# Last stage of a spectral-layer backward pass: half-width inverse DFT sums, interleaved layer-norm rows, x reloaded elsewhere

## The chip, the cores and the metric

One core of one Trainium2 chip. The metric is the device time of one execution in microseconds (us); lower is better. The kernel was tuned already, so changes of one or two per cent count, and an execution's own spread (364.7 to 368.5 us over three batches of the kernel before) is of the size of the smaller effects. "PE" is TensorE, "PEld" its weight loads, "DVE" VectorE, "ACT" ScalarE, "POOL" GpSimd, "SP" SyncE, which issues the DMAs. A *cast* below is the copy of a PSUM result to SBUF in bf16.

## The reference

A residual block with two branches, and all of its gradients (shapes S = 2048 rows, D = 448 columns, F = 1792):

```python
h  = x + irfft2(rfft2(layernorm(x)) * (w_r + 1j * w_i))           # branch A, bf16
h2 = h + transpose(gelu(layernorm(layernorm(h)) @ w1 + b1) @ w2 + b2)   # branch B, mixes rows (cut: axes left out)
outputs = h2, and the gradients of x, w_r, w_i, w1, b1, w2, b2 for grad_out
```

What matters here is the end of the backward pass. The gradient of x needs an inverse DFT along the rows (sixteen tiles of 128 x 448), then the backward of the layer norm on each tile. Beside it the kernel does large matmuls for the gradients of w1 and w2 as *fill work*, handed to PE in small steps between the row work.

## The kernel before

Three pieces count. The row DFT gives four matmuls of 448 columns a tile, with `n_fill` steps of gradient work ahead of them:

```python
for s1 in range(NT):                       # NT = 16 row tiles
    if s1 + ahead_ < NT:
        q.append(first(s1 + ahead_))       # four 128-column matmuls and one cast prepare a later tile
    aT = q.pop(0)
    fill(n_fill)                           # n_fill = 8 gradient steps
    py = ps_ff()                           # a PSUM tile
    for i in range(4):                     # i // 2: cosine or sine part
        mm(py[:, 0:D], lhsT=aT[0:KC, i, :], rhs=csI[0:KC, i // 2, i % 2, :],
           start=(i == 0), stop=(i == 3))
    consumer(s1, py)
```

The consumer is the layer norm's backward, per tile one ACT operation, four DVE operations and small POOL operations on single columns:

```python
sc.activation(out=pb, in_=ps, func=ACT.Identity, scale=rstd, accum_out=ms)          # ACT, 448 columns
ve.tensor_tensor_reduce(out=tmp, in0=pb, in1=nrm, ..., accum_out=m2)                # DVE
...                                                                                 # cut: POOL works out s1, s2
ve.tensor_scalar(out=tmp, in0=nrm, scalar1=s2, scalar2=s1, op0=ALU.mult, op1=ALU.add)
ve.tensor_tensor(out=pb, in0=pb, in1=tmp, op=ALU.add)
ve.tensor_tensor(out=pb, in0=pb, in1=resid, op=ALU.add)                             # then stored, one tile a DMA
```

A cast goes to ACT or DVE, whichever has the lower load in a *cost model* that adds up an estimated duration for each operation as the program is built:

```python
def cost(self, name, n, bf16):
    if self.i == 0:                        # ACT
        return 0.17 + n / 1250.0
    if name in (..., "scalar_tensor_tensor", "tensor_tensor_reduce") or name == "tensor_copy" and not bf16:
        return 0.1 + n / 960.0             # DVE
    ...
    return 0.06 + n / (rate * (2.0 if bf16 else 1.0))
```

Of the kernel before, what the change touches and what calls it, by code (L numbers as in the profile page):

```python
# [13 lines left out]
ALU = mybir.AluOpType  # L14
# [3 lines left out]
P = 128  # L18
# [21 lines left out]
N_FILL_B = (16, 16, 40, 8, 24, 8)  # L40
# [10 lines left out]
class Meter:  # L51
# [10 lines left out]
    def cost(self, name, n, bf16):  # L62
        if self.i == 0:
            return 0.17 + n / 1250.0
        if name in ("bn_stats", "scalar_tensor_tensor", "tensor_tensor_reduce") or name == "tensor_copy" and not bf16:
            return 0.1 + n / 960.0
        rate = {"tensor_tensor": 960.0, "tensor_scalar": 1920.0, "tensor_copy": 1920.0}.get(name, 960.0)
        return 0.06 + n / (rate * (2.0 if bf16 else 1.0))

    def __getattr__(self, name):  # L70
        fn = getattr(self.eng, name)

        def run(**kw):
            ap = kw["in_"] if "in_" in kw else kw["in0"]
            n = int(np.prod(ap.shape[1:]))
            self.load[self.i] += self.cost(name, n, ap.dtype == BF16)
            low = max(self.load) - Meter.slack
            self.load[0], self.load[1] = max(low, self.load[0]), max(low, self.load[1])
            fn(**kw)  # L79
            side = Meter.side  # L80
            Meter.count += self.i
            if side and self.i == 1 and Meter.count % Meter.every == 0:
                Meter.side = ()
                side.pop(0)()
                Meter.side = side
        return run
# [33 lines left out]
def kernel(  # L120
# [634 lines left out]
    def inv_rows(consumer, n_fill, aTs, on_dve=()):  # L755
# [17 lines left out]
        for s1 in range(NT):  # L773
            if s1 + ahead_ < NT:
                q.append(first(s1 + ahead_))
            aT = q.pop(0)
            fill(n_fill)
            py = ps_ff()
            for i in range(4):
                mm(py[:, 0:D], lhsT=aT[0:KC, i, :], rhs=csI[0:KC, i // 2, i % 2, :],  # L780
                                 start=(i == 0), stop=(i == 3))
            consumer(s1, py)

    pending = []

    def fill(n):
        while n > 0 and pending:
            try:
                next(pending[0])
                n -= 1  # L790
            except StopIteration:
                pending.pop(0)

    def drain():
        while pending:
            fill(1)
# [367 lines left out]
    gp_.tensor_scalar(out=xcol[:, 2, :], in0=mvx[:, :, 0], scalar1=-1.0 / D, scalar2=None, op0=ALU.mult)  # L1164

    def ln_a(i, ps, rstd, nrm, m2scale):
# [3 lines left out]
        gp_.tensor_scalar(out=m1, in0=ms, scalar1=-1.0 / D, scalar2=None, op0=ALU.mult)  # L1170
        ve.tensor_tensor_reduce(out=tmp, in0=pb, in1=nrm, scale=-m2scale, scalar=0.0,
# [27 lines left out]
    ahead = []  # L1199

    def st_load():
        if order:
            reg, j = order.pop(0)
            st = st_ring.next()
            nc.sync.dma_start_transpose(out=st, in_=reg[:, j * 1024 + 64:j * 1024 + 960])
            ahead.append(st)


# [7 lines left out]
    for t in range(NT):  # L1216
# [10 lines left out]
        if t >= NT - 2:  # L1227
            st_load()
# [25 lines left out]
    def gw_gen(n, rhs, width, store, ost):  # L1254
        for u in range(n // 2):
            st = ahead.pop(0)
# [9 lines left out]
            def out(pw, w, c, i):  # L1266
# [3 lines left out]
                if x:  # L1270
                    if c == 3 and i:
                        st_load()
                    defer(1.5, lambda j=2 * u + i: store(j, 512 * (c - 1), x + w, o), o)

            for c in range(0, 4, 2):
# [14 lines left out]
                for i in range(2):  # L1290
                    for k in range(3):
                        whole(pv, w, c + 1, i, k, False, k == 2)
                        if k == 2:
# [7 lines left out]
                          Ring(ring(rG, 0, 8, S // 2).views + ost.views)))  # L1301
    load_W(3)
    for t in range(NT - LAG, NT + 2):
        if t == NT - 2:
            fill(8)
        rows(t)
# [7 lines left out]
    xall = cut(rX, 0, NT, D)  # L1314

    def load_xall(q):
        nc.sync.dma_start(out=xall[:, 4 * q:4 * q + 4, :], in_=x_pt[:, 4 * q:4 * q + 4, :])

    load_xall(0)
    load_xall(1)  # L1320

    X_AT = {3: 2, 7: 3}
    GW_AT = (4, 9, 11, 11, 12, 13, 14, 15)

    def gx_consumer(t, py):
# [4 lines left out]
        pb, tmp, m1, m2, ms = ln_a(NT + t, py[:, 0:D], rstd_x[:, t:t + 1], xall[:, t, :], 1.0 / D)  # L1330
        u, s2, s1 = (gcol[:, t, k:k + 1] for k in range(3))
        nmean, rstd2, md = (xcol[:, k, t:t + 1] for k in range(3))
        gp_.tensor_scalar(out=u, in0=ms, scalar1=md, scalar2=None, op0=ALU.mult)
        gp_.tensor_scalar(out=s2, in0=m2, scalar1=u, scalar2=rstd2, op0=ALU.subtract, op1=ALU.mult)
        gp_.tensor_scalar(out=s1, in0=s2, scalar1=nmean, scalar2=m1, op0=ALU.mult, op1=ALU.add)
        gx_todo.append((t, pb, tmp, s1, s2))
        if len(gx_todo) > 1:
            gx_finish()

    gx_todo = []  # L1340

    def gx_finish():
        t, pb, tmp, s1, s2 = gx_todo.pop(0)
        ln_b(pb, tmp, s1, s2, xall[:, t, :], dh[:, t, :], pb)
        defer(2.0, lambda: nc.sync.dma_start(out=out_1[0].rearrange("(p t) d -> p t d", t=NT)[:, t, :], in_=pb), pb)

    inv_rows(gx_consumer, N_FILL_B[5], aT_ring)
    while gx_todo:
        gx_finish()
    drain()  # L1350
    for _ in g_out:
        pass
# [30 lines left out]
```

## Time and profile before

366.0 us (median of three, 365.92 to 366.91). The span, first to last instruction, is 365.5.

| | before |
|---|---|
| PE busy, share of the span | 348.1 us, 95% |
| DVE busy | 262.2 us, 72% |
| ACT busy | 206.0 us, 56% |
| last stage starts, PE (first group of 128-column matmuls) | 309.89 us |
| last matmul group ends | 360.30 us |
| tail from there to the end of the span | 5.2 us |

The slices, stretches and chain are read in the prediction. One line of the page that it did not use matters afterwards. It is the clock that PE was granted, in tenths of full speed, one digit for each fortieth of the span:

```profile
PEclk9699998999999999999999999999999999999999
```

The 8 in the seventh slice (54.8 to 64.0 us, the eye takes it for noise) is a stretch of 3.41 us at half clock: in the clock record 1.00 is granted until 60.31, 0.50 until 63.73 and 1.00 after it.

### The profile page before, as it was taken

Reading aid. Unit: us, or ns where it says so; the run is one execution under the profiler, and the core shown is the slowest. Engines: PE = TensorE matmul, PEld = TensorE weight load, DVE = VectorE, ACT = ScalarE, POOL = GpSimd, SP = SyncE. Lnnn points to the kernel's source line nnn. Section 1 sums busy time; section 2 is a strip of 40 time slices with the busy share of each in tenths; the row PEclk is TensorE's granted clock in tenths of the full one; section 3 lists DMA queues with packets and bytes.
Section 4 is the critical chain, followed back from the end, with each engine's and each line's share of the span. In section 5 each row is a group of like instructions: output and inputs, shape, how many; then the busy total and the mean of one; then the engine's idle time right before and its main releaser. Section 6 shows DMA issues by size and latency. Waiting matters only on the chain.

```text
span 365.5 us, 6419 instructions
## 1 busy us (share of the span) xinstructions
PE 348.1 (95%) x2133; PEld 184.5 (50%) x2133; DVE 262.2 (72%) x677; ACT 206.0 (56%) x427; POOL 70.4 (19%) x226
## 2 busy tenths in 40 slices
PE   6798997899999999999999999999999999999994
PEld 2365764555645555555555555543444444455541
DVE  5898738882884888594237887874787884589882
ACT  4668834965986454512222455564577674676662
POOL 8676000000220000001001111100000000376760
PEclk9699998999999999999999999999999999999999
DMA  8999999647999999976868999969578899788897
GB/s 201 285 197 242 192 204 187 133 119 255 279 292 360 305 339 225 256 223 193 207 162 168 200 166 245 193 185 230 184 204 225 231 203 266 233 224 268 191 216 244
DMA packets 148825, 81.63 MB, mean 223 GB/s; under 512 B 95608, under 2 KB 140920, under 8 KB 148536
## 3 DMA queue, kind: packets, MB, share of 16 engines
q1 hardware_dynamic: 148792, 81.23, 91.7%
q8 instruction: 16, 0.26, 0.3%
q14 instruction: 17, 0.14, 0.1%
HBM read 27.56 MB, written 23.89 MB: 141 GB/s over the span
## 4 chain that ended last, share of the span: by engine, by line
PE 81%; ACT 5%; DVE 4%; DMA 3%; issue 2%; POOL 2%; SPq 1%; ACTq 0%; DVEq 0%
PE ps_mm L215 66%; PE ps_ff L215 15%; DMA rO<-in_B_w_dram 2%; ACT rO L79 2%; ACT rG L79 1%; DMA rA<-in_A_x_dram 1%; DVE stats L79 1%; DVE r L79 1%; SPq L294 1%; ACT Ut L79 1%; DVE rA L79 1%; ACT rX L79 0%; DVE rS L79 0%; POOL nt_f L383 0%; ACT rAT L79 0%
## 5 line engine op out<-in xcount | busy, mean ns | idle before, releaser
L215 PEld LDWEIGHTS <-r 128*128 128x128 bf16 (+1 forms) x628 | 59.9, 105 | 49.2 <-issue 2.0
L215 PEld LDWEIGHTS <-rS 128*128 128x128 bf16 (+2 forms) x528 | 42.9, 98 | 41.4 <-issue 9.2
L1170 POOL TENSOR_SCALAR lcol<-lcol 128x1 f32<-128x1 f32 x32 | 18.0, 562 | 148.4 <-ACT r L79 148.4
L215 PE MATMUL ps_mm<-rD,r 128*128 128x448 bf16 x224 | 44.5, 352 | 0.0
L215 PE MATMUL ps_mm<-rC,rE 128*128 128x448 bf16 x144 | 36.2, 369 | 3.7 <-DMA rC<-in_grad_out_dram 3.1
L215 PEld LDWEIGHTS <-rst 128*128 128x128 bf16 (+1 forms) x320 | 23.8, 97 | 29.0 <-issue 13.2
L79 ACT CAST rO<-ps_mm 128x512 bf16<-128x512 f32 (+1 forms) x52 | 28.5, 583 | 14.6 <-PE ps_mm L215 12.7
L79 ACT CAST r<-ps_ff 128x452 bf16<-128x452 f32 x53 | 30.5, 577 | 8.4 <-PE ps_ff L215 7.8
L215 PE MATMUL ps_mm<-rG,rst 128*128 128x512 bf16 (+1 forms) x160 | 35.0, 380 | 0.0
L215 PE MATMUL ps_mm<-rB,r 128*128 128x448 bf16 x160 | 31.2, 352 | 0.1
L215 PE MATMUL ps_mm<-r,rst 128*128 128x512 bf16 (+3 forms) x160 | 31.2, 353 | 0.0
L79 DVE CAST rO<-ps_mm 128x512 bf16<-128x512 f32 (+1 forms) x28 | 18.1, 658 | 10.4 <-PE ps_mm L215 10.3
L215 PE MATMUL ps_ff<-csI,rAT 113*128 113x448 bf16 x108 | 24.9, 353 | 0.4 <-ACT rAT L79 0.2
L79 DVE SCALAR_TENSOR_TENSOR r<-ps_mm,b2col,r 128x448 bf16<-128x448 f32 x16 | 10.9, 682 | 19.9 <-PE ps_mm L215 18.1
L79 ACT ACTIVATE r<-ps_mm,rstd_h 128x448 bf16<-128x448 f32 x16 | 10.1, 633 | 26.1 <-PE ps_mm L215 26.1
L79 ACT ACTIVATE r<-rC 128x448 bf16<-128x448 bf16 x16 | 9.1, 571 | 26.7 <-DMA out_dram<-r 19.3
L215 PEld LDWEIGHTS <-rO 128*128 128x128 bf16 (+1 forms) x165 | 15.8, 99 | 13.1 <-DMA rO<-in_B_w_dram 2.5
L215 PE MATMUL ps_mm<-rC,rO 128*128 128x448 bf16 x80 | 20.0, 366 | 2.2 <-DMA rO<-in_B_w_dram 2.2
L79 ACT ACTIVATE rG<-rG 128x896 bf16<-128x896 bf16 x14 | 13.3, 950 | 14.9 <-DVE rG L79 14.7
L215 PE MATMUL ps_mm<-rE,rS 128*128 128x448 bf16 x112 | 21.5, 352 | 0.0
L79 ACT CAST rS<-ps_ff 128x512 bf16<-128x512 f32 x31 | 18.3, 589 | 3.9 <-PE ps_ff L215 3.7
L215 PEld LDWEIGHTS <-rE 128*128 128x128 bf16 x148 | 14.2, 100 | 11.9 <-issue 4.8
(191 smaller groups left out, 634.4 us busy)
## 6 DMA issues: line engine op xcount, KB each, us to landing
out_dram<-rO SPq DMA_DIRECT2D x34, 256.0 KB
r<-in_B_w_dram SPq DMA_DIRECT2D x5, 1024.0 KB
r<-r SPq DMA_DIRECT2D x16, 226.0 KB
r<-r SPq DMA_DIRECT2D x32, 113.0 KB
rS<-in_B_w_dram SPq DMA_DIRECT2D x4, 896.0 KB
out_dram<-r SPq DMA_DIRECT2D x32, 112.0 KB
out_dram<-rG SPq DMA_DIRECT2D x10, 256.0 KB
rO<-in_B_w_dram SPq DMA_DIRECT2D x2, 1024.0 KB
```

What stands on the lines that cost most here:

```text
L79: fn(**kw)
L215: nc.tensor.matmul(out, lhsT=lhsT, rhs=rhs, start=start, stop=stop)
L294: nc.sync.dma_start_transpose(out=wT, in_=B_w2[j * P:(j + 1) * P, :].rearrange("f (t c) -> f t c", c=P))
L1170: gp_.tensor_scalar(out=m1, in0=ms, scalar1=-1.0 / D, scalar2=None, op0=ALU.mult)
```

## The change

Intent: an inverse DFT of real data is symmetric up to sign. With E the sum over cosines and O the sum over sines for the first 224 columns, column d is E + O and the mirrored column is E - O. So PE needs half of the columns, and ACT and DVE put the two halves together.

```diff
-N_FILL_B = (16, 16, 40, 8, 24, 8)
+N_FILL_B = (16, 16, 40, 8, 24, 9)
...  cost model: ACT 0.17 + n/1250 -> 0.12 + n/1200 (+0.1 with accumulator); DVE 0.1 -> 0.13, 0.06 -> 0.16 or 0.18
             for i in range(4):
+                if halves_:
+                    o = i // 2 * (D // 2)
+                    mm(py[:, o:o + D // 2], lhsT=aT[0:KC, i, :], rhs=csI[0:KC, i // 2, i % 2, 0:D // 2],
+                       start=(i % 2 == 0), stop=(i % 2 == 1))
+                    continue
...  in fill(n), after each step:
+                if row_ops:
+                    row_ops.pop(0)()
...  transposed tiles of the gradient work: one more buffer, each loaded one unit earlier
-    X_AT = {3: 2, 7: 3}
-    GW_AT = (4, 9, 11, 11, 12, 13, 14, 15)
+    X_AT = {0: 2, 4: 3}                      # x goes into the freed gelu region, two loads before the middle stage
+    GW_AT = (1, 3, 5, 6, 7, 9, 11, 12)       # stores of the spectral weights' gradients
...  the consumer (its POOL operations cut here); own rings of 8 + 8 row tiles, stores of two tiles at a time
+        def scaled_sum():
+            sc.activation(out=tmp[:, 0:h], in_=py[:, 0:h], func=ACT.Identity, scale=rstd, accum_out=ms)
+        def low():
+            ve.scalar_tensor_tensor(out=pb[:, 0:h], in0=py[:, h:D], scalar=rstd, in1=tmp[:, 0:h],
+                                    op0=ALU.mult, op1=ALU.add)
+        def high():
+            ve.scalar_tensor_tensor(out=pb[:, h:D], in0=py[:, D - 1:h - 1:-1], scalar=nrstd_x[:, t:t + 1],
+                                    in1=tmp[:, h - 1::-1], op0=ALU.mult, op1=ALU.add)
...  products, line, add_line, finish: the four DVE operations of before
+        now = [scaled_sum, low, high, products]
+        row_ops.append(now.pop(0))
+        old = held_ops.pop(0) if len(held_ops) == 2 else []
+        while now or old:
+            for ops in (now, old):
+                if ops:
+                    row_ops.append(ops.pop(0))
+        held_ops.append([line, add_line, finish])
```

More of the change, by code (lines that the diff above doesn't have):

```diff
@@ L63, in cost @@
         if self.i == 0:
-            return 0.17 + n / 1250.0
+            return 0.12 + n / 1200.0
         if name in ("bn_stats", "scalar_tensor_tensor", "tensor_tensor_reduce") or name == "tensor_copy" and not bf16:
-            return 0.1 + n / 960.0
+            return 0.13 + n / 960.0
+        base = {"tensor_tensor": 0.16}.get(name, 0.18)
         rate = {"tensor_tensor": 960.0, "tensor_scalar": 1920.0, "tensor_copy": 1920.0}.get(name, 960.0)
-        return 0.06 + n / (rate * (2.0 if bf16 else 1.0))
+        return base + n / (rate * (2.0 if bf16 else 1.0))
     def __getattr__(self, name):
@@ L76, in run @@
             self.load[self.i] += self.cost(name, n, ap.dtype == BF16)
+            if not self.i and 'accum_out' in kw:
+                self.load[0] += 0.1
             low = max(self.load) - Meter.slack
@@ L753, in s2_inv, with inv_rows @@
         defer(RESH_LAG, lambda: nc.sync.dma_start(out=D3[rowbase(g):rowbase(g) + 29:4, :, :, :], in_=ab), ab)
-    def inv_rows(consumer, n_fill, aTs, on_dve=()):
+    def inv_rows(consumer, n_fill, aTs, on_dve=(), halves_=False):
         def first(s1):
@@ L782, in inv_rows @@
             consumer(s1, py)
-    pending = []
+    pending, row_ops = [], []
     def fill(n):
@@ L1163 @@
     gp_.tensor_tensor(out=xcol[:, 1, :], in0=rstd_x[:], in1=rstd_x[:], op=ALU.mult)
-    gp_.tensor_scalar(out=xcol[:, 2, :], in0=mvx[:, :, 0], scalar1=-1.0 / D, scalar2=None, op0=ALU.mult)
+    gp_.tensor_scalar(out=xcol[:, 2, :], in0=mvx[:, :, 0], scalar1=-2.0 / D, scalar2=None, op0=ALU.mult)
     def ln_a(i, ps, rstd, nrm, m2scale):
@@ L1170, in ln_a, with ln_halves @@
         gp_.tensor_scalar(out=m1, in0=ms, scalar1=-1.0 / D, scalar2=None, op0=ALU.mult)
+        ve.tensor_tensor_reduce(out=tmp, in0=pb, in1=nrm, scale=-m2scale, scalar=0.0,
+                                op0=ALU.mult, op1=ALU.add, accum_out=m2)
+        return pb, tmp, m1, m2, ms
+    nrstd_x = nmr_h
+    gp_.tensor_scalar(out=nrstd_x[:], in0=rstd_x[:], scalar1=-1.0, scalar2=None, op0=ALU.mult)
+    def ln_halves(i, ps, rstd, nrm, m2scale):
+        h = D // 2
+        pb, tmp = (r448[:, s * D:(s + 1) * D] for s in ((i % NT) % 6, 6 + i % 2))
+        ms, m1, m2 = (lcol[:, i, k:k + 1] for k in range(3))
+        sc.activation(out=tmp[:, 0:h], in_=ps[:, 0:h], func=ACT.Identity, scale=rstd, accum_out=ms)
+        gp_.tensor_scalar(out=m1, in0=ms, scalar1=-2.0 / D, scalar2=None, op0=ALU.mult)
+        k = i % NT
+        ve.scalar_tensor_tensor(out=pb[:, 0:h], in0=ps[:, h:D], scalar=rstd, in1=tmp[:, 0:h], op0=ALU.mult, op1=ALU.add)
+        ve.scalar_tensor_tensor(out=pb[:, h:D], in0=ps[:, D - 1:h - 1:-1], scalar=nrstd_x[:, k:k + 1],
+                                in1=tmp[:, h - 1::-1], op0=ALU.mult, op1=ALU.add)
         ve.tensor_tensor_reduce(out=tmp, in0=pb, in1=nrm, scale=-m2scale, scalar=0.0,
@@ L1198, with st_load, load_xall @@
     order = [(rE, j) for j in range(NFB // 2)] + [(rB, t) for t in range(NT // 2)]
-    ahead = []
-    def st_load():
-        if order:
-            reg, j = order.pop(0)
-            st = st_ring.next()
-            nc.sync.dma_start_transpose(out=st, in_=reg[:, j * 1024 + 64:j * 1024 + 960])
-            ahead.append(st)
+    st_at = [st_ring.views[n if n < 3 else (n - 4) % 3] for n in range(15)]
+    st_at[3] = cut(r448, NG * P, 7, P)
+    st_next = iter(st_at)
+    def st_load(n):
+        if n < 15:
+            reg, j = order[n]
+            nc.sync.dma_start_transpose(out=st_at[n], in_=reg[:, j * 1024 + 64:j * 1024 + 960])
+    xall = cut(rE, 0, NT, D)
+    def load_xall(q):
+        nc.sync.dma_start(out=xall[:, 4 * q:4 * q + 4, :], in_=x_pt[:, 4 * q:4 * q + 4, :])
     def rows(t):
@@ L1226 @@
             fold_quarters(dh, t // 2)
-        if t >= NT - 2:
-            st_load()
+        if t >= NT - 3:
+            st_load(t - NT + 3)
         if t == 3:
@@ L1252, with gw_gen @@
     o4 = out_4.rearrange("(p t) f -> p t f", t=NT)
-    def gw_gen(n, rhs, width, store, ost):
-        for u in range(n // 2):
-            st = ahead.pop(0)
+    def gw_gen(n, rhs, width, store, ost, u0=0):
+        for u in range(u0, u0 + n // 2):
+            st = next(st_next)
             def whole(pw, w, c, i, k, start, stop):
@@ L1270, in out @@
                 if x:
-                    if c == 3 and i:
-                        st_load()
-                    defer(1.5, lambda j=2 * u + i: store(j, 512 * (c - 1), x + w, o), o)
+                    if c == 3 and i and u != 3:
+                        st_load(u + 4 if u < 3 else u + 3)
+                    defer(1.5, lambda j=2 * (u - u0) + i: store(j, 512 * (c - 1), x + w, o), o)
             for c in range(0, 4, 2):
@@ L1300 @@
                           lambda t, a, n, o: nc.sync.dma_start(out=o4[:, t, a:a + n], in_=o[:, 0:n]),
-                          Ring(ring(rG, 0, 8, S // 2).views + ost.views)))
+                          Ring(ring(rG, 0, 8, S // 2).views + ost.views), NFB // 2))
     load_W(3)
     for t in range(NT - LAG, NT + 2):
+        if t == 13:
+            st_load(3)
+        if t == 14:
+            load_xall(0)
+        if t == 16:
+            load_xall(1)
         if t == NT - 2:
@@ L1313 @@
     g_out = w_io(W_view_B, out_2, out_3, True)
-    xall = cut(rX, 0, NT, D)
-    def load_xall(q):
-        nc.sync.dma_start(out=xall[:, 4 * q:4 * q + 4, :], in_=x_pt[:, 4 * q:4 * q + 4, :])
-    load_xall(0)
-    load_xall(1)
-    X_AT = {3: 2, 7: 3}
-    GW_AT = (4, 9, 11, 11, 12, 13, 14, 15)
+    X_AT = {0: 2, 4: 3}
+    GW_AT = (1, 3, 5, 6, 7, 9, 11, 12)
     def gx_consumer(t, py):
@@ L1329, in gx_consumer @@
             next(g_out, None)
-        pb, tmp, m1, m2, ms = ln_a(NT + t, py[:, 0:D], rstd_x[:, t:t + 1], xall[:, t, :], 1.0 / D)
+        pb, tmp = (r448[:, t % 8 * D:(t % 8 + 1) * D], r452[:, t % 8 * D:(t % 8 + 1) * D])
+        ms, m1, m2 = (lcol[:, NT + t, k:k + 1] for k in range(3))
         u, s2, s1 = (gcol[:, t, k:k + 1] for k in range(3))
         nmean, rstd2, md = (xcol[:, k, t:t + 1] for k in range(3))
-        gp_.tensor_scalar(out=u, in0=ms, scalar1=md, scalar2=None, op0=ALU.mult)
@@ L1334, in gx_consumer @@
-        gp_.tensor_scalar(out=s2, in0=m2, scalar1=u, scalar2=rstd2, op0=ALU.subtract, op1=ALU.mult)
-        gp_.tensor_scalar(out=s1, in0=s2, scalar1=nmean, scalar2=m1, op0=ALU.mult, op1=ALU.add)
-        gx_todo.append((t, pb, tmp, s1, s2))
-        if len(gx_todo) > 1:
-            gx_finish()
-    gx_todo = []
-    def gx_finish():
-        t, pb, tmp, s1, s2 = gx_todo.pop(0)
-        ln_b(pb, tmp, s1, s2, xall[:, t, :], dh[:, t, :], pb)
-        defer(2.0, lambda: nc.sync.dma_start(out=out_1[0].rearrange("(p t) d -> p t d", t=NT)[:, t, :], in_=pb), pb)
@@ L1347 @@
-    inv_rows(gx_consumer, N_FILL_B[5], aT_ring)
-    while gx_todo:
-        gx_finish()
+        rstd, xt, h = rstd_x[:, t:t + 1], xall[:, t, :], D // 2
+        def scaled_sum():
+            sc.activation(out=tmp[:, 0:h], in_=py[:, 0:h], func=ACT.Identity, scale=rstd, accum_out=ms)
+            gp_.tensor_scalar(out=m1, in0=ms, scalar1=-2.0 / D, scalar2=None, op0=ALU.mult)
+            gp_.tensor_scalar(out=u, in0=ms, scalar1=md, scalar2=None, op0=ALU.mult)
+        def low():
+            ve.scalar_tensor_tensor(out=pb[:, 0:h], in0=py[:, h:D], scalar=rstd, in1=tmp[:, 0:h],
+                                    op0=ALU.mult, op1=ALU.add)
@@ new lines, in high, with products @@
+        def high():
+            ve.scalar_tensor_tensor(out=pb[:, h:D], in0=py[:, D - 1:h - 1:-1], scalar=nrstd_x[:, t:t + 1],
+                                    in1=tmp[:, h - 1::-1], op0=ALU.mult, op1=ALU.add)
+        def products():
+            ve.tensor_tensor_reduce(out=tmp, in0=pb, in1=xt, scale=-1.0 / D, scalar=0.0,
+                                    op0=ALU.mult, op1=ALU.add, accum_out=m2)
+            gp_.tensor_scalar(out=s2, in0=m2, scalar1=u, scalar2=rstd2, op0=ALU.subtract, op1=ALU.mult)
+            gp_.tensor_scalar(out=s1, in0=s2, scalar1=nmean, scalar2=m1, op0=ALU.mult, op1=ALU.add)
@@ new lines, in line, with add_line, finish @@
+        def line():
+            ve.tensor_scalar(out=tmp, in0=xt, scalar1=s2, scalar2=s1, op0=ALU.mult, op1=ALU.add)
+        def add_line():
+            ve.tensor_tensor(out=pb, in0=pb, in1=tmp, op=ALU.add)
+        def finish():
+            ve.tensor_tensor(out=pb, in0=pb, in1=dh[:, t, :], op=ALU.add)
+            if t % 2:
+                s = (t - 1) % 8
+                defer(2.0, lambda: nc.sync.dma_start(
+                    out=out_1[0].rearrange("(p t) d -> p t d", t=NT)[:, t - 1:t + 1, :], in_=cut(r448, s * D, 2, D)))
@@ L1350 @@
+        now = [scaled_sum, low, high, products]
[6 more added lines that the diff above has]
+        held_ops.append([line, add_line, finish])
+    held_ops = []
+    inv_rows(gx_consumer, N_FILL_B[5], aT_ring, (), True)
+    while held_ops:
+        row_ops.extend(held_ops.pop(0))
     drain()
+    while row_ops:
+        row_ops.pop(0)()
```

## The prediction

> **What bounds the kernel now.** I read the page's slices first, then the busy times by stretch, the chain of waits, and the timeline of the last stage.
>
> ```profile
> PE   6798997899999999999999999999999999999994
> DVE  5898738882884888594237887874787884589882
> ACT  4668834965986454512222455564577674676662
> ...
> PE 81%; ACT 5%; DVE 4%; DMA 3%; issue 2%; POOL 2%; SPq 1%; ACTq 0%; DVEq 0%
> ```
>
> TensorE is full from the tenth slice on, and the chain that ended last runs 81% through it. The last stage by stretches (time, then busy us and count of PE, PEld, DVE, ACT, POOL, then clock and DMA share):
>
> ```profile
> 310.00:350.00 40.00, 40.00 (x264) 20.43 (x263) 31.68 (x83) 27.03 (x64) 24.30 (x56) 1.00 0.86 228
> 350.00:366.00 16.00, 10.30 (x59) 4.39 (x56) 7.70 (x18) 5.73 (x14) 3.62 (x9) 0.94 0.79 224
> ```
>
> PE has no hole in 310 to 350 at full clock. DVE is at 79%, ACT at 68%. In the list of PE's waits nothing appears after 242.4 us. So the end is set by PE's instruction stream plus a tail: the last matmul group ends at 360.31, the span at 365.5. That tail of 5.2 us is one evacuation (0.42), the SP queue's last output issues (361.59 to 362.70) and their landing. The reported time is 366.0, 0.5 over the span.
>
> **One row of the last stage now.** The timeline gives one row's PE work and its neighbours (start, duration):
>
> ```profile
> 332.33 0.62 DVE L79 CUSTOM_DVE_ANT_0 r<-r,rX 128x448 bf16<-128x448 bf16 x1
> 332.88 0.08 DVE L79 DVE_READ_ACCUMULATOR2_ANT lcol<- 128x1 f32 x1
> 332.88 0.39 DVE L79 TENSOR_SCALAR r<-rX,stats 128x448 bf16<-128x448 bf16 x1
> 333.30 0.39 DVE L79 TENSOR_TENSOR r<-r 128x448 bf16<-128x448 bf16 x1
> 333.32 0.92 PE L215 MATMUL ps_ff<-csI,rAT 113*128 113x448 bf16 x4
> 333.73 0.42 DVE L79 TENSOR_TENSOR r<-r,rA 128x448 bf16<-128x448 bf16 x1
> 334.07 0.68 DVE L79 CAST rG<-ps_mm 128x512 bf16<-128x512 f32 x1
> 334.08 0.39 PE L215 MATMUL ps_ff<-RTm,r 128*113 128x128 bf16 x4
> ```
>
> Four matmuls of 448 columns form the row (0.76 us from 333.32 to the next group at 334.08, so 0.19 each), four of 128 prepare the next, then 8 steps of the weight-gradient product fill in. Sixteen rows from 310.06 to 352.52 are 2.65 us a row; the 40 steps left over drain from 352.52 to 360.31, that is 0.195 us a step. On DVE, start to start, a row costs 0.55 (product with accumulator) + 0.42 + 0.43 + 0.34 = 1.74 us, the rest being evacuations.
>
> [...]0.19 for 448 above, and the 226-column matmuls of the stage before start 0.10 apart (301.54, 301.64). [...]casts from PSUM take 0.68 us at 512 and 0.41 at 256 columns, 1.05 ns a column[...]. [...]I therefore use starts, not busy time, and they show a dense stream. [...]In this trace the folds of the first stage read one operand backwards and still take 0.38 us for 448 bf16 columns, like forward adds (0.39); I give the backward read no penalty.
>
> **The change part by part.**
>
> PE. The cosine half and the sine half are now separate sums of 224 columns: four matmuls of 224 for four of 448. At 0.19 less 0.097 that saves 0.093 each, 0.373 a row, 16 x 0.373 = 5.97 us. Nothing else leaves PE. The ninth fill step only moves 16 steps from the drain into the rows: new row 2.65 - 0.373 + 0.195 = 2.47 us (from the pieces 9 x 0.195 + 0.21 + 0.39 = 2.36; between the two lie the switches between groups), and the drain falls from 40 steps to 24, 7.8 to 4.7 us. If PE never waits it ends at 360.31 - 5.97 = 354.3.
>
> ACT. The scaled copy goes from 448 to 224 columns. Its 0.63 us (0.53 plus 0.10 for the accumulator read, start to start) becomes about 0.44, at 0.83 ns a column from casts of 512 and 256 (0.59 and 0.38). With the cast of the transposed row (0.46 start to start) that is 0.90 a row. A pair of gradient blocks is 28 steps and eight evacuations, six of 512 columns (0.47) and two of 256 (0.26), 3.34 us; nine steps are 9/28 of that, 1.07 a row. ACT with every evacuation: 1.97 of 2.47 us.
>
> DVE. Two scalar-tensor-tensor operations of 224 columns are added. The 448-column form elsewhere in this kernel takes 0.68 and lets the next start after 0.59 (160.29 to 160.88). Less 224 columns at 1.04 ns, that is 0.36 each, 0.72 a row and 11.5 us in all. The other four operations stay; with rows interleaved, neighbours no longer depend on each other, so the 0.42 and 0.43 should come near 0.34: 0.55 + 3 x 0.34 = 1.57. Sum 2.29 us a row, without one evacuation, and 1.74 + 0.72 = 2.46 if the overlap is not won.
>
> Balance. The changed cost model makes DVE dearer and ACT cheaper. By it a row's DVE work counts 2 x 0.363 + 0.597 + 0.297 + 2 x 0.393 = 2.41, ACT's own work 0.95, all evacuations 1.26; so nearly every evacuation will be given to ACT, where there is room. The same model governs every stage. Outside DMA, PE waits for ACT or DVE before the last stage add up to a few us (1.7, 0.9, 0.7 the longest); I take the net effect of other choices there as 0 +- 1.
>
> Loads. x goes into the released gelu region; two of four loads move to before the middle stage. At present 1.2 us of DVE waiting is for this load; PE does not wait for it, so the time gains nothing directly. The stage does lose two 448 KB reads while it gets shorter, which about cancels for DMA. Output rows go out in pairs, 8 issues for 16, and the gradient outputs of the spectral weights start earlier, so the SP queue at the end should be no fuller. Tail kept at 5.2, plus 0.2 for denser DMA.
>
> Sum: 365.5 - 5.97 + 0.8 (PE waits from a DVE that is 93 to 99% full in the rows) + 0.2 = 360.5 span, 361.0 reported. The 0.8 is my estimate: about 0.05 a row, between no stall and the full DVE pace.
>
> **The rivals.**
> A: PE still sets the end and takes everything: 366.0 - 6.0 = 360.0, and up to 1 us less if the emptier SP queue shortens the tail. For it: two rows of slack for each statistic, four PSUM buffers in each group, ACT at 80%.
> B: DVE becomes the bound. If a row costs 2.6 us (full durations 2 x 0.45 + 0.62 + 0.08 + 3 x 0.39 come to 2.77, overlap takes some back) or some evacuations stay on it, PE waits for PSUM and the row falls back to about 2.65. Then only the shorter drain is left: 16 x 0.195 = 3.1 us, 363 us. For it: DVE grows by 11.5 us on an engine 79% busy. Against: measured starts, not durations, and the cost model unloads it.
> C: DMA sets the end. Its share is 0.86 over 310 to 350, and 0.99 in 359 to 362. Six us less for the same stores would leave the tail longer, 362 to 364. Against: [...]x loads moved out, and shares over 1.0 occur in stretches where PE never waits, so the share is no hard limit.
> D: other stages get worse by the new balance or by earlier x loads ahead of the gather transfers; 366 or more only if this exceeds 5 us, while the fill of 9.7 us of matmuls after the gathers (247.08 to 256.8) covers a late one.
>
> **Range and chances.** Weights about 0.45 for A with small stalls, 0.3 for B in part, 0.2 for C, 0.05 for D. Middle 361.0; 358.9 needs all of PE's gain and a shorter tail with some luck in other stages, 364.2 is B and C together. Two per cent faster is 358.7 or less, beyond what PE's own arithmetic gives: 0.08. Slower than 373.3: 0.02. Within 2%: 0.90.
>
> **What would show it.** Right: ps_ff matmuls of 224 columns 0.10 us apart; row pace 2.4 to 2.5; PE without waits for ps_ff or ps_mm in the rows; nearly all casts of the rows on ACT; DVE near full; drain about 4.7 us; start of the stage near 310. Wrong: row pace 2.6 or more with PE waiting for DVE (B); last matmul near 354 but the span more than 6 us later (C); stage start moved by more than 1 us (D, or luck of the balance); the backward operation slower than the forward one, or either over 0.5 us.

365.5 - 5.97 + 0.8 + 0.2 comes to 360.5, and with 0.5 to 361.0. The trace of before has, from one start to the next, a median of 97 ns for 226 columns and of 189 for 448 (128-row operands); by these alone the saving is 0.092 a matmul, 0.37 a row and 5.9 us in all. DVE's 1.04 ns a column is 1.05 by the casts, which leaves 0.36 as it is. The 0.8 and the 0.2 are estimates; for the 0.2 no working is given. A DMA share over 1.0 while PE never waits is, for instance, the 1.10 of 310 to 312 us, with PE busy 2.00 of 2.00.

## The result, and the profile after

The changed kernel took 359.84 us (median of four, 359.38 to 360.36) against 366.14 (365.92 to 366.91) for the kernel before in the same comparison. The ratio is 0.9825, 95% interval 0.9802 to 0.9848: 6.3 us faster. (A ratio is the mean time of one kernel's fast runs over that of the other's of the same rounds, so not quite the ratio of the medians quoted.)

The slices after, and the shares of the chain that ended last:

```profile
PE   5888998899999999999999999999999999999994
...
DVE  5896626991884888685327888784497766489895
ACT  4659836965986555503221455565478776478883
...
PEclk9699999999999999999999999999999999999999
...
PE 76%; DVE 8%; ACT 7%; DMA 4%; issue 3%; SPq 1%; POOL 0%; ACTq 0%; DVEq 0%
```

PE is as full as before from the tenth slice on. ACT is busier in the last ten slices, and DVE's share of the final chain has doubled, from 4% to 8%. The clock line has lost its 8. The last stage by stretches (columns as in the prediction):

```profile
309.00:349.00 40.00, 40.00 (x296) 22.61 (x298) 33.64 (x100) 31.92 (x84) 18.24 (x58) 1.00 1.04 248
```

DVE rose from 79% to 84% of the stretch and ACT from 68% to 80%, and PE still has no hole (busy 40.00 of 40.00 us). One row's new work, from the timeline (start, duration, engine, operation, in square brackets the idle time before it and what ended it):

```profile
312.96 0.45 ACT L82 ACTIVATE r<-ps_ff,rstd_x 128x224 bf16<-128x224 f32 x1
...
313.54 0.45 DVE L82 SCALAR_TENSOR_TENSOR r<-ps_ff,rstd_x,r 128x224 bf16<-128x224 f32 x1
...
313.90 0.44 DVE L82 SCALAR_TENSOR_TENSOR r<-ps_ff,nmr_h,r 128x224 bf16<-128x224 f32 x1
...
316.29 0.55 PE L218 MATMUL ps_ff<-csI,rAT 113*128 113x224 bf16 x4
...
316.68 0.39 PE L218 MATMUL ps_ff<-RTm,r 128*113 128x128 bf16 x4
```

Four matmuls of 224 columns take 0.39 us from their start to the next group's, 0.097 each. The two new DVE operations start 0.36 us apart, and the backward read (the second, scalar `nmr_h`) costs no more than the forward one (means of 443 and 450 ns over the stage).

The end of the stage, DVE's last operations and the last DMA issues:

```profile
353.68 0.39 DVE L82 TENSOR_TENSOR r<-r,r 128x448 bf16<-128x448 bf16 x1
354.11 0.39 DVE L82 TENSOR_TENSOR r<-r,rA 128x448 bf16<-128x448 bf16 x1
354.53 0.33 SPq L1394 DMA_DIRECT2D out_dram<-r  x1
354.98 0.85 SPq L1331 DMA_DIRECT2D out_dram<-rG  x2
```

The last row's final add ends at 354.50, 1.2 us after the last matmul group (353.27), and the store of that row follows at once. Before, the last piece of the chain was a cast on DVE (0.42 us from 360.34).

**Where the 7.0 us of span went.** For every run, the span of its profiled execution splits into three parts: the start of the last stage on PE, PE's time in it, and the tail.

| kernel | stage starts | last matmul ends | PE in the stage | tail | span |
|---|---|---|---|---|---|
| before | 309.89 | 360.30 | 50.41 | 5.2 | 365.5 |
| after | 308.99 | 353.27 | 44.28 | 5.2 | 358.5 |
| b_newmeter | 306.28 | 356.66 | 50.38 | 5.5 | 362.2 |
| b_filler | 307.80 | 358.20 | 50.40 | 6.0 | 364.2 |
| b_halves | 308.87 | 358.66 | 49.79 | 6.3 | 365.0 |
| b_ring | 308.56 | 357.75 | 49.19 | 7.2 | 365.0 |
| b_gw | 308.71 | 357.90 | 49.19 | 5.2 | 363.1 |
| a_oldmeter | 310.45 | 354.71 | 44.26 | 5.5 | 360.2 |
| a_flat | 308.54 | 352.80 | 44.26 | 5.9 | 358.7 |
| a_dve | 307.48 | 351.76 | 44.28 | 9.0 | 360.8 |
| a_xold | 307.22 | 351.48 | 44.26 | 6.3 | 357.8 |
| a_best | 309.48 | 352.66 | 43.18 | 5.0 | 357.7 |

(a_gw's only profile is slow, and a_narrow is not a clean test; both are told below.) Between before and after, PE's time in the stage fell by 6.13 us, the start came 0.90 earlier, and the tail did not move. The 0.90 is two things that partly cancel, and neither is a lasting effect. First, the half clock near 60 us, gone after. PE's timeline there, before and after (the same fourteen matmuls lie between the first and the last line):

```profile
60.43 0.93 PE L215 MATMUL ps_mm<-rC,rO 128*128 128x448 bf16 x2 [2.17 <-DMA rO<-in_B_w_dram]
...
64.33 0.35 PE L215 MATMUL ps_ff<-r,Vt 128*128 128x452 bf16 x1
```

```profile
60.57 0.55 PE L218 MATMUL ps_mm<-rC,rO 128*128 128x448 bf16 x2 [1.39 <-DMA rO<-in_B_w_dram]
...
62.86 0.35 PE L218 MATMUL ps_ff<-r,Vt 128*128 128x452 bf16 x1
```

They took 3.90 us before and 2.29 after, 1.61 less. Second, PE waits once at the start of the last stage, which it did not before:

```profile
308.99 0.63 PE L218 MATMUL ps_ff<-RTm,r 128*113 128x128 bf16 x8 [0.80 <-PE ps_mm L218]
```

The releaser named is PE itself, so the true one is not identified. The SP queue suggests a gather of rows through DRAM that was issued late, behind a transpose whose issue alone took 2.93 us:

```profile
302.57 2.93 SPq L1233 DMA_TRANSPOSE rst<-rB  x1
305.60 0.62 SPq L756 DMA_DIRECT2D r<-r  x1
```

Two runs with the same code ahead of this point, a_flat and a_dve, have no such wait, and their stages start at 308.54 and 307.48. So both belong to single executions. Only the 6.13 us of the stage repeats, in a_oldmeter, a_flat, a_dve and a_xold to within 0.02 us.

### The profile page after: what moved, and what is told of

It reads as the page before. It is cut to its first block, busy times and chain, and to the rows that moved or that the text cites. A ratio compares the mean times of both kernels' runs of the same rounds, so it can differ in the third digit from the quotient of the medians.

```text
span 358.5 us, 6455 instructions
## 1 busy us (share of the span) xinstructions
PE 341.3 (95%) x2133; PEld 183.5 (51%) x2133; DVE 252.4 (70%) x676; ACT 214.9 (60%) x460; POOL 64.0 (18%) x227
## 4 chain that ended last, share of the span: by engine, by line
PE 76%; DVE 8%; ACT 7%; DMA 4%; issue 3%; SPq 1%; POOL 0%; ACTq 0%; DVEq 0%
PE ps_mm L218 63%; PE ps_ff L218 13%; DVE r L82 4%; DMA rO<-in_B_w_dram 2%; ACT rO L82 2%; DVE stats L82 2%; DMA rA<-in_A_x_dram 1%; ACT rG L82 1%; ACT Ut L82 1%; DVE rA L82 1%; DVE rS L82 1%; SPq L297 1%; ACT r L82 1%; ACT Vt L82 1%; ACT rX L82 0%
## 5 line engine op out<-in xcount | busy, mean ns | idle before, releaser
L218 PEld LDWEIGHTS <-r 128*128 128x128 bf16 (+2 forms) x660 | 61.7, 104 | 50.8 <-issue 3.8
L218 PEld LDWEIGHTS <-rS 128*128 128x128 bf16 (+2 forms) x496 | 40.3, 98 | 39.3 <-issue 7.6
L82 ACT CAST rO<-ps_mm 128x512 bf16<-128x512 f32 (+1 forms) x63 | 33.7, 576 | 12.5 <-PE ps_mm L218 12.1
L82 ACT CAST r<-ps_ff 128x452 bf16<-128x452 f32 x58 | 33.5, 577 | 8.6 <-PE ps_ff L218 8.2
L218 PE MATMUL ps_mm<-r,rst 128*128 128x512 bf16 (+3 forms) x192 | 36.6, 353 | 0.0
L218 PE MATMUL ps_mm<-rG,rst 128*128 128x512 bf16 (+1 forms) x128 | 28.2, 380 | 0.0
L82 DVE CAST rO<-ps_mm 128x512 bf16<-128x512 f32 x17 | 11.6, 689 | 16.3 <-PE ps_mm L218 15.4
L82 ACT CAST rG<-ps_mm 128x512 bf16<-128x512 f32 (+1 forms) x35 | 17.2, 540 | 6.9 <-PE ps_mm L218 6.7
L1180 POOL TENSOR_SCALAR lcol<-lcol 128x1 f32<-128x1 f32 x16 | 8.5, 532 | 65.1 <-ACT r L82 65.1
L218 PE MATMUL ps_ff<-csI,rAT 113*128 113x224 bf16 (+1 forms) x108 | 19.0, 298 | 0.4 <-ACT rAT L82 0.2
```

What stands on the lines that cost most here:

```text
L82: fn(**kw)
L218: nc.tensor.matmul(out, lhsT=lhsT, rhs=rhs, start=start, stop=stop)
L1180: gp_.tensor_scalar(out=m1, in0=ms, scalar1=-1.0 / D, scalar2=None, op0=ALU.mult)
```

## The experiments

Twelve kernels ran, in three batches, with the kernel before on the same chip in each batch (medians 366.97, 366.95 and 365.81). Names starting with b_ are the kernel before with something added; those starting with a_ are the changed kernel with something undone. All are correct unless said.

### b_newmeter: the new cost model alone

```diff
-            return 0.17 + n / 1250.0
+            return 0.12 + n / 1200.0
...  and the other constants of the new model
```

> The kernel before with the new cost model alone; last stage, loads and fill untouched. Theory (some 1.9 us of the gain arose before the last stage, because the rebalanced forward stage reaches a weight tile later, waits 1.4 us for its load in place of 2.2, and so escapes a 3.4 us stretch at half clock): the stretch at half clock near 60 us is gone or shorter, the last stage starts 1 to 2 us earlier, time 364.2 to 365. Rival (the cost model is worth nothing by itself and the earlier start came from chance or the moved loads): 366.0 to 366.4, half clock as before.

Measured: 365.39 us (363.96 to 367.57), ratio 0.9969 (0.9936 to 1.0003). By the ratio 1.1 us, between what theory and rival said, with an interval from 2.3 us to no change. PE's time in the last stage is that of before (50.38). In its profile the stage started at 306.28, the earliest of all, without a half clock near 60 us (PE waited 0.91 there); but the same kernel's six runs spread over 3.6 us.

### a_oldmeter: the changed kernel with the old cost model

```diff
-            return 0.12 + n / 1200.0
+            return 0.17 + n / 1250.0
...  and the other constants of the old model
```

> The changed kernel with the old cost model. Theory: the half-clock stretch near 60 us returns (about +1.8 us), the last stage keeps its 5.97 us since 9 casts of it go back to DVE, which has 0.25 us a row free; 361.5 to 362.2. Rival (without the cost model DVE is overfull and PE waits for it): row pace over 2.5 us, time 363 or more.

Measured: 362.06 us (359.83 to 363.36), ratio 0.9871 (0.9836 to 0.9906). Slower than the changed kernel's 0.9825 in its own comparison by about 1.7 us (0.0046 of 366), with intervals that just overlap. More than half of this lies outside the span: four of its six executions take 3.0 to 3.5 us longer than their spans and the other two 2.1, the changed kernel's 1.75 to 1.83, which makes 1.1 us on average. What fills that time no view shows. The loss that the span has is not in the last stage: PE's time there is 44.26, without a wait. Of some 50 casts of gradient work in the stage DVE did 11 here, 4 in the changed kernel, 16 in b_newmeter and 22 in the kernel before. So most casts left DVE because the new row work fills DVE's account, in either cost model. What lengthened the span of this profile lies earlier: the stage began at 310.45, and the half clock near 60 us is back.

```profile
60.83 0.93 PE L215 MATMUL ps_mm<-rC,rO 128*128 128x448 bf16 x2 [2.23 <-DMA rO<-in_B_w_dram]
```

### b_filler: keep PE busy in the wait near 60 us

```diff
             pg = ps_mm()
+            if j == 9:                       # the wait for the weights' DMA falls here
+                scratch = ps_ff()
+                for _ in range(10):
+                    nc.tensor.matmul(scratch[:, 0:D], lhsT=ident[:], rhs=go_tp[:, 0, :], start=True, stop=True)
```

> The kernel before with ten matmuls of 448 columns into a scratch accumulator (1.9 us) placed just ahead of the matmuls that wait 2.2 us for a weight tile at 58 to 60 us; nothing reads them. Theory (the idle wait itself costs a half-clock stretch after it): no half clock near 60 us, 1.4 to 1.8 us less, 364.3 to 364.8, although PE does more work. Rival (the half clock is not due to this wait): 366.0 to 366.5.

Measured: 366.19 us (365.49 to 368.13), ratio 0.9989 (0.9962 to 1.0017). Its profile has no half clock near 60 us (two matmuls take 0.39 us from 60.14, start to next start, against 0.72 from 60.43 in before; the mean granted clock is 0.989), and its stage starts at 307.80 instead of 309.89. Yet the time over all runs did not move clearly; it lies in the rival's range. So the dip cost the profiled execution of before some 1.6 us, and it explains little of the difference between the medians. Whether it occurs varies from run to run: it followed waits of 2.17 and 2.23 us in the profiles of before and a_oldmeter, but not those of 2.13, 2.14 and 2.47 in the profiles of b_gw, b_ring and b_halves. So the length of the wait alone does not tell whether it occurs; what does was not shown. In the clock records of before and after, the stretches between two changes are 3.413, 6.827, 44.373, 3.413 and 300.373 us, and 3.413, 6.827 and 341.333, each within 0.04 us of a whole multiple of 3.413; the dip is the second 3.413 of before.

### b_halves: the half sums alone

```diff
-inv_rows(gx_consumer, N_FILL_B[5], aT_ring)
+inv_rows(gx_consumer, N_FILL_B[5], aT_ring, (), True)      # four matmuls of 224 columns
...  consumer: ACT on 224 columns, two DVE sums, the other four DVE operations at once and as before
...  eight row tiles shared by pb and tmp, x loads, stores, transposes and cost model of before
```

> The kernel before with only the half-column sums: 224-column matmuls, a scaled copy of half the columns, two scalar-tensor-tensor operations; old cost model, old order of row operations, eight fill steps, x where it was. Theory (PE's own work is the gain and DVE keeps up without the rest): 366.1 - 6.0 = 360.1, up to 361. Rival (the interleaving and the rebalancing are needed): PE waits for PSUM in the rows, pace over 2.4 us a row in place of 2.27, 362 or more.

Measured: 365.98 us (364.64 to 366.79), ratio 0.9977 (0.9951 to 1.0003). The matmuls are as cheap as in the changed kernel, and nearly nothing of it reaches the end: PE's time in the stage is 49.79, not 44.28. DVE falls behind PE. The same operation in two rows, one after the other:

```profile
339.10 0.62 DVE L79 CUSTOM_DVE_ANT_0 r<-r,rX 128x448 bf16<-128x448 bf16 x1
341.67 0.62 DVE L79 CUSTOM_DVE_ANT_0 r<-r,rX 128x448 bf16<-128x448 bf16 x1
```

A row costs DVE 2.57 us here, while PE's row groups come 2.29 us apart (311.24 to 340.97 over thirteen rows): 0.28 us a row. That is rival B of the prediction, a row of 2.6 us on DVE; in the changed kernel, with rows interleaved, a row takes DVE 2.17 us. Later the chain runs through stores as well (start, length, what the chain waits on):

```profile
341.11 3.09 DMA out_dram<-r
...
347.59 5.44 DMA out_dram<-r
```

DVE wrote into these row tiles again only after the store had landed. The numbers are lengths of stores; DVE itself waited 0.82 and 0.37 us for them, so the next expectation, which calls 3.1 and 5.4 us waits, reads them wrongly. PE waits for other things, all but 0.46 us of it from 341 us on (waited-for, us in total, times, longest):

```profile
PE ps_mm L215 <- DMA rst<-rB: 1.7, 1, 1.7
...
PE ps_mm L215 <- ACT rG L79: 1.1, 2, 0.7
PE ps_mm L215 <- DVE rG L79: 0.9, 1, 0.9
PE ps_mm L215 <- ACT rO L79: 0.5, 1, 0.5
```

The first is a transposed tile for the gradient work; the others are PSUM tiles that wait for a cast. Together 4.2 us. This is the most useful run: the prediction's PE arithmetic was right and would have been worth almost nothing without the rest of the change.

### b_ring: the half sums with 8 + 8 row tiles

```diff
-        pb, tmp, h = m448.next(), m448.next(), D // 2
+        pb, tmp, h = pb_ring.next(), tmp_ring.next(), D // 2   # rings of eight each
```

> The half-column sums alone on the kernel before, as in the run that gained nothing, with one thing more: eight tiles each for a row's result and its scratch in place of eight shared by both, so a tile comes round after eight rows, not four. Theory (in that run VectorE and ScalarE sat waiting 3.1 and 5.4 us for output stores to leave a row tile before writing it again; the tiles held PE up): those waits vanish, last stage as short as in the changed kernel, 361 to 362.5 beside 366 to 367 of before. Rival (the stores are simply too slow for the shorter stage, DMA is the bound): the wait moves to the next buffer, 364 or more.

Measured: 367.01 us (365.95 to 368.95), ratio 1.0001 (0.9972 to 1.0029). No gain: the waits for row stores are gone from the chain, and the transposed tile takes their place.

```profile
336.77 6.43 DMA rst<-rB
```

That is one transpose, from its issue to its landing; PE waits 1.8 us of it. The rival was right here: row tiles were one limit of several, and lifting it alone shortens PE's stage by 0.6 us (49.19) and not the time. A row still costs DVE 2.57 us. At the end SP's queue is busy without a break from 354.96 to 361.31, and the tail is 7.2 us.

### b_gw: b_ring with the spectral gradients stored early

```diff
-    GW_AT = (4, 9, 11, 11, 12, 13, 14, 15)
+    GW_AT = (1, 3, 5, 6, 7, 9, 11, 12)
```

> The kernel before with the half sums, eight row tiles of each kind instead of eight shared ones, and the gradient stores of the spectral weights issued early; x reloaded as before, casts chosen as before. Theory (queue and buffers at the end swallow the gain): the waits for the transposes of the last blocks go and 3 to 4 us come back, 362 to 364 us. Rival (these stores are not it): 366 us or more, with the same waits of PE for the transposed tiles near 340 us.

Measured: 365.55 us (364.12 to 367.89), ratio 0.9986 (0.9947 to 1.0026). The rival again. The tail of this one execution is back at 5.2 us (a_flat and a_xold, which store early too, have 5.9 and 6.3), but PE's time in the stage did not change (49.19). The waits of PE, and the transpose behind the first of them in SP's queue:

```profile
PE ps_mm L215 <- DMA rst<-rB: 1.9, 1, 1.9
PE ps_mm L215 <- ACT rG L79: 1.1, 2, 0.7
PE ps_mm L215 <- ACT rO L79: 0.5, 1, 0.5
```

```profile
337.18 3.60 SPq L1210 DMA_TRANSPOSE rst<-rB  x1
```

Its issue alone took 3.60 us, and SP's next issue started at 340.88, after it; the transpose landed at 343.4, and one more transpose follows at 346.12 (issue 1.23 us). In the changed kernel the corresponding last transposes are out of the way early:

```profile
333.78 2.71 SPq L1233 DMA_TRANSPOSE rst<-rB  x1
```

No transpose comes after that one, though PE uses the tiles till 353 us: the changed kernel has one more buffer for them and loads each a unit ahead. This was a part of the diff that the prediction did not mention. The waits listed in b_gw add to 3.5 us of the 4.9 by which its stage is longer than the changed kernel's; the rest stands in the trace as PE busy time (45.60 against 44.28 us), and I have no cause for it. I did not run the kernel before with this part added, so that it is the missing piece is argued from the wait and not shown.

### a_narrow: the changed kernel with 4 + 4 row tiles (wrong result)

```diff
-        pb, tmp = (r448[:, t % 8 * D:(t % 8 + 1) * D], r452[:, t % 8 * D:(t % 8 + 1) * D])
+        pb, tmp = (r448[:, t % 4 * D:(t % 4 + 1) * D], r452[:, t % 4 * D:(t % 4 + 1) * D])
...
-                s = (t - 1) % 8
+                s = (t - 1) % 4
```

> The changed kernel with four tiles each for result and scratch in place of eight. Theory (store landing in this stretch takes more than four rows at times): VectorE waits for output stores, 1.5 to 5 us lost, 361.5 to 365. Rival (the earlier gradient stores and paired row stores relieve DMA enough, the number of tiles does not matter): 359.5 to 361.

Measured: 373.70 us (371.56 to 375.88), ratio 1.0170 (1.0134 to 1.0206), and a wrong gradient of x (relative error 0.5). That was not intended: the stores of pairs are deferred in program order, and with four tiles a pair is overwritten before its store is emitted. DVE waited 16.1 us for stores of row tiles, six times, and PE's stage took 56.02 us. The size fits the theory that the number of row tiles matters, but a run that does not compute the right thing carries little weight, and I build nothing on it.

### a_flat: the changed kernel without interleaving

```diff
         held_ops.append([line, add_line, finish])
+        while row_ops:
+            row_ops.pop(0)()
```

> The changed kernel with the operations of a row issued all at once after its matmuls, not one by one between the gradient steps. Theory (VectorE has 0.25 us a row to spare and hardly any cast to do): 359.5 to 361, within 0.7 of the changed kernel. Rival (a burst of seven operations in front of a cast makes PE wait for PSUM): PE waits for casts of VectorE, 362 or more.

Measured: 360.07 us (359.55 to 361.93), ratio 0.9809 (0.9781 to 0.9836): the same as the changed kernel. All of a row's operations are handed out at once instead of one for each gradient step, and PE still never waits in the stage. So spreading them is not needed. Holding a row's last three operations back by two rows was left in place, so that half of the interleaving is not tested. With it a row still takes DVE as little as 2.17 us here (340.79 to 342.96), so the holding, and not the spreading, may be what brings it down from 2.57.

### a_dve: one of the two new DVE operations done twice

```diff
         def products():
+            high()
             ve.tensor_tensor_reduce(out=tmp, in0=pb, in1=xt, scale=-1.0 / D, ...)
```

> The changed kernel with the backward scalar-tensor-tensor done twice in each row, 0.33 us more on VectorE, same result. Theory (a row takes VectorE 2.17 us and PE 2.42): 2.50 a row makes VectorE the bound by 0.1 us a row and lengthens its run-out after the last row, in all 1 to 3 us, 361 to 363. Rival (VectorE has more room than that): no change, 359.5 to 360.5. Rival (VectorE is already the bound): all of 16 x 0.33 = 5.3 us, 365.

Measured: 362.88 us (362.23 to 364.43), ratio 0.9888 (0.9864 to 0.9913), 2.3 us over the changed kernel's ratio. A row costs DVE 2.66 us now (345.47 to 348.13 between the accumulating operations of two rows), 0.49 more than in the changed kernel, where 0.33 was expected, and more than PE's pace of 2.42. Even so PE does not wait once in the stage (44.28 us). The whole cost comes after it:

```profile
356.34 0.39 DVE L82 TENSOR_TENSOR r<-r,rA 128x448 bf16<-128x448 bf16 x1
```

```profile
356.76 0.33 SPq L1395 DMA_DIRECT2D out_dram<-r  x1
357.21 0.86 SPq L1331 DMA_DIRECT2D out_dram<-rG  x2
```

DVE's last add ends 5.0 us after PE's last matmul, against 1.2 in the changed kernel. Here the slower DVE shows up as a longer run-out, not as stalls of PE in the rows; in sixteen rows the backlog did not reach PE.

### a_gw: the changed kernel with late stores of the spectral gradients

```diff
-    GW_AT = (1, 3, 5, 6, 7, 9, 11, 12)
+    GW_AT = (4, 9, 11, 11, 12, 13, 14, 15)
```

> The changed kernel with one part undone: the gradient stores of the spectral weights are issued as late as in the kernel before. Theory: at the end of the last stage the DMA queue and the buffers behind it are what swallowed the gain of the half sums when they came alone, and storing these gradients early is what makes room. Then the tail after the last matmul grows from 5.2 us and stores are waited for near 340 us: 362 to 364 us. Rival: the time of these stores doesn't matter (the reload of x into gelu tiles or the casts made the difference): 359.5 to 361 us, tail 5 to 5.5 us.

Measured: 361.50 us as the median of six, of which the profiled one is slow (506.25 us, clock 0.656); the five fast runs are 360.66 to 362.88, ratio 0.9871 (0.9835 to 0.9907). In the same batch a_xold has 0.9847 and a_best 0.9808. By these ratios late stores cost some 1 to 2 us, between what theory and rival said, but the intervals overlap, so the loss is not shown; and without a fast profile I can't say where it would lie.

### a_xold: the changed kernel with x read in the last stage, as before

```diff
-    xall = cut(rE, 0, NT, D)
+    xall = cut(rX, 0, NT, D)
...
-    X_AT = {0: 2, 4: 3}
+    X_AT = {3: 2, 7: 3}
```

> The changed kernel with another part undone: x is read again in the last stage into tiles of its own, as before, not early into freed gelu tiles. Theory (the DMA at the end is what matters): two reads of 448 KB are back in the stage, the DMA share of the last 40 us rises, and the time with it by 0.5 to 2 us: 360.4 to 362 us. Rival (the reads are covered): no change, 359.5 to 360.5 us.

Measured: 359.96 us (358.49 to 362.77), ratio 0.9847 (0.9802 to 0.9892). No difference that the runs could show. The reads are covered: DVE waits 0.9 us for one of them, PE not at all (44.26). Moving x bought nothing that these runs show.

### a_best: an attempt to beat both

```diff
-N_FILL_B = (16, 16, 40, 8, 24, 9)
+N_FILL_B = (16, 16, 40, 8, 29, 8)       # five more gradient steps before the stage, one fewer in each row
```

> The changed kernel with five more work items placed ahead of the last stage, where PE waits 0.8 us, and one fewer per step in the last stage's rows, so that DVE has its row work done nearer to PE's end. Theory (PE's new wait of 0.8 us is a gap that work can fill, and DVE's run-out sets the tail): 358.5 to 359.5 us, no wait of PE at the start of the stage. Rival (the wait is for a transfer whose time moves with the queue, and the tail is set by the stores): 359.5 to 360.5 us.

Measured: 359.27 us (358.38 to 360.05), ratio 0.9808 (0.9777 to 0.9840). Its profile shows what was intended. The stage starts without a wait:

```profile
309.48 0.61 PE L218 MATMUL ps_ff<-RTm,r 128*113 128x128 bf16 x8
```

PE's time in it is 1.10 us less, because five steps lie ahead of it, and DVE's row work is done at 352.15, before PE's end at 352.66, where it was 1.2 us after it. The intervals of the two ratios overlap widely, so no gain is shown; by the ratios it would be 0.6 us. What is left of the tail, 5.0 us, is casts (DVE until 353.08), issues (SP until 354.49) and landing (span end 357.7).

## Why the prediction was right

It said 361.0 with a range of 358.9 to 364.2; 359.84 was measured, and "within 2%" at 0.90 came true, if near the line. Step by step:

- **PE, "16 x 0.373 = 5.97 us".** Right. The matmuls start 0.097 us apart (0.39 for four) as forecast, and PE's time in the stage fell by 6.13; the rest of 0.16 was not traced. The drain took 5.02 us for 4.7 predicted, and the row pace is 2.45 for 2.47, measured as there (308.99 to 348.25, sixteen rows); between the row groups alone it is 2.42 (311.61 to 347.86 over fifteen rows).
- **"0.8 (PE waits from a DVE that is 93 to 99% full in the rows)".** Wrong. DVE was 84% busy, a row cost it 2.17 us start to start (345.54, 347.72, 349.88) instead of 2.29, since a 448-column operation with one of another row behind it lets the next start after 0.30 to 0.31 us (345.91, 346.21; 346.57, 346.87; 347.41, 347.72) where 0.34 was assumed. And a_dve shows that PE does not wait for DVE in the changed kernel even with 2.66 us a row. There DVE's load is paid in the run-out: its last add ends 5.0 us after PE's last matmul, against 1.2 in the changed kernel. So rival B falls for the changed kernel. For the half sums alone its first half came true (2.57 us a row in b_halves), and there PE did wait 0.9 us for a cast on DVE.
- **"Tail kept at 5.2, plus 0.2".** The size was right (5.2), its making was not: DVE's last row (until 354.50), not the last cast, is what it waits for. (With DVE done before PE, in a_best, the tail is 5.0 all the same.)
- **"Net effect of other choices there as 0 +- 1".** The profiled spans have 0.90 here, made up of a half-clock stretch that went and a wait that came, both of single executions. Over all runs the new cost model is worth about 1 us by b_newmeter and 1.7 by a_oldmeter, of which 1.1 lie outside the span; neither interval is clear of no effect. I leave its size open.
- **"Nearly every evacuation will be given to ACT".** Right in its result (44 of 48 casts of gradient work), but the reason was only half right: with the old model 40 of 51 go there as well.
- **"0.5 over the span".** A slip. It compares the median time with the span of an execution that took 367.3. The right difference is 1.8 us, and the span that belongs to the median is about 364.2. The two errors above (0.8 too much for stalls, 0.2 for the tail) and the 0.9 of the start made the predicted span of 360.5 too long by 2.0 against 358.5; the slip of 1.3 the other way hid much of it, so that the time came out too long by 0.75 for the profiled execution (360.25) and by 1.2 for the median. That the middle lies so near is in part luck.
- **Loads and stores: "the time gains nothing directly", "should be no fuller".** For x this is what a_xold shows. For the rest the step was mis-sized. Rival C, that DMA gives the gain back, was described and set at 0.2; it is just what happens when the half sums come alone (b_halves, b_ring, b_gw), through row tiles that wait for stores (DVE waits 0.82 and 0.37 us in b_halves) and a transposed tile that lands late (PE waits 1.7 to 1.9 us in the three), with a DVE that is slower than PE (rival B; 2.57 us a row against 2.29 in b_halves). The parts of the change that look like housekeeping are the ones that let 6 us through. Of these, the second set of row tiles is not enough alone, nor with the early stores; the spreading (a_flat), the moved x (a_xold) and the ninth step in each row (a_best) can each be taken back without a loss that shows; the earlier transposes, the paired stores and the two-row holding were never added to the kernel before, or taken back, one by one. Which of them is needed stays open.

The gain of the medians, 6.30 us, is thus PE's 6.13 and nothing else that these runs could separate from the spread.

## What to carry to other kernels

Shortening the engine that sets the end was worth its arithmetic here only once the buffers and transfers that keep it fed could follow: PE's stage lost 0.62 us with the half sums alone (b_halves) and 6.13 with the whole change. Look in the stage for what is loaded or stored at a fixed distance in work, since it comes due earlier when the work shrinks. An engine beside it that gets slower than it need not stall it over a short stage (a_dve: 2.66 us a row on DVE, 2.42 on PE, sixteen rows, no wait of PE); ask how long that engine runs on after the last matmul, and whether anything that the first engine needs stands in its queue. Before explaining a difference of a microsecond between two traces, split the span into the same parts in several runs and keep only what repeats, and convert a span to a time with the time of that very execution.
